# Chunked attention and a squared-ReLU layer on one core: q and k transposes issued together, and the attention output transposed by DMA from the sixth group on

## The chip, the core and the metric

The kernel runs on one core of a Trainium2 chip. A core has TensorE (PE, matmuls; its weight loads, PEld, run beside them), VectorE (DVE), ScalarE (ACT), GpSimd (POOL) and SyncE (SP, which here only issues DMAs). The engines run side by side and wait for each other through semaphores. The metric is the device time in microseconds (us), a median over runs.

## What is computed

Attention within chunks of 64 tokens, then a two-layer network on every token:

```python
# q, k, v: (8 batches, 8 heads, 576 tokens, 64), float32
scores = scale * q_chunk @ k_chunk.T            # per head, chunk by chunk: 64 x 64
attn   = softmax(scores)
x      = (attn @ v_chunk) as (4608 tokens, 8 heads * 64 = 512)
h      = maximum(x @ w_in, 0)                   # w_in 512 x 2048
out    = (h * h) @ w_out                        # w_out 2048 x 512, out (4608, 512) float32
```

## The kernel before, in words

**Groups and blocks.** The 4608 tokens are cut into 18 groups of 256 (two tiles of 128 tokens, t = 0 and 1). Attention is done by group, the network by block: block 0 is groups 0 to 2, blocks 1 to 7 are the pairs (3,4) to (15,16), block 8 is group 17. While a block runs through the network, the attention of the next block's groups is done in between.

**The four steps of a group's attention** (`T, SC, AV, XT` in the code):
- T, `transpose_qk`: TensorE transposes 8 pieces of q (128 x 128 each, through the identity matrix `ident`) into one half of a PSUM tile, DVE copies that half to SBUF (`qkT`); TensorE transposes 8 pieces of k into the other half, ACT copies it. The inputs are float32; the transposes read the upper two bytes of each value as bf16.
- SC, `scores`: 64 x 64 matmuls of k and q into a PSUM tile; ACT writes the exponential `e`.
- AV, `values`: for each t, matmuls of `e` with v (v carries a column of ones, which gives the sums), then on DVE a reciprocal `rec` and a multiplication, giving `x`, 128 tokens x 512 in bf16.
- XT, `transpose_x`: TensorE transposes 8 pieces of `x` into a PSUM tile, and DVE copies it into `xT` (128 features x 4 x tokens), the layout in which the network's first matmul wants it.

**The network.** `ffn_in` takes 16 steps (`ft`); each is four matmuls into a PSUM tile `ps_ffn`, a ReLU on ACT (`rl`) and a square on DVE (`gT`). `ffn_out` takes, per tile of 128 tokens, 16 matmuls into a `ps_ffn` tile, a copy on ACT (`o_sb`) and a store.

**What sets the order.** The code is written in the order in which each engine executes it; nothing reorders it afterwards. A dictionary `plan` says after which slot of a block (a slot is one `ft` of `ffn_in`, or four matmuls of `ffn_out`) which attention steps are issued; a pair block has slots 0 to 31. Each engine works through its own instructions in order, so an instruction that waits holds up those behind it on that engine. All DMAs are issued by SP, in order. At the head of block j SP issues the loads of block j+2; the stores follow in the order of the code.

**Buffers.** Attention's PSUM tiles, `ps_att`, rotate over 2 buffers; `ps_ffn` over 4; `x` over 6; `xT` over 2; `o_sb` over 4; q and k over 5 groups.

Of the kernel before, what the change touches and what calls it, by code (L numbers as in the profile page):

```python
# [10 lines left out]
BF16 = mybir.dt.bfloat16  # L11
# [5 lines left out]
def kernel(  # L17
# [9 lines left out]
    nc = tc.nc  # L27
# [6 lines left out]
    n_hp = H // 2  # L34
    n_dt = d_model // 128
    n_ft = d_ff // 128
    GT = 256
    n_grp = n_tokens // GT
    blocks = [[0, 1, 2]] + [[g, g + 1] for g in range(3, n_grp - 1, 2)] + [[n_grp - 1]]
    BT = GT * max(len(b) for b in blocks)  # L40

    const_pool = ctx.enter_context(tc.tile_pool(name="const", bufs=1))
# [3 lines left out]
    att_pool = ctx.enter_context(tc.tile_pool(name="att", bufs=3))  # L46
# [20 lines left out]
    def segments(g0, n):  # L67
        while n:
            b, s = divmod(g0, S)
            m = min(n, S - s)  # L70
            yield b, s, m
            g0 += m
            n -= m
# [3 lines left out]
    def load_qk(g):  # L77
        q_sb = in_pool.tile([128, 2, H, D], FP32, name="q_sb")
        k_sb = in_pool.tile([128, 2, H, D], FP32, name="k_sb")
        qk[g] = (q_sb, k_sb)  # L80
        for t in range(2):
            for dst, src in ((q_sb, q), (k_sb, k)):
                p = 0
                for b, s, m in segments(g * GT + t * 128, 128):
                    nc.sync.dma_start(  # L85
                        out=dst[p:p + m, t, :, :],
                        in_=src[b, :, s:s + m, :].rearrange("h s d -> s h d"))
                    p += m

    def load_v(g):  # L90

        vt = v_tiles[g % NV]
        for t in range(2):
            g0 = g * GT + t * 128
            p = 0
            for b, s, m in segments(g0, 128):
                nc.sync.dma_start(  # L97
                    out=vt[p:p + m, t, 0::2, 0:D],
                    in_=v[b, 0::2, s:s + m, :].rearrange("h s d -> s h d"))
                p += m  # L100
            for half in range(2):
                b, s = divmod(g0 + 64 * half, S)
                p = 64 * (1 - half)
                nc.sync.dma_start(  # L104
                    out=vt[p:p + 64, t, 1::2, 0:D],
                    in_=v[b, 1::2, s:s + 64, :].rearrange("h s d -> s h d"))

    def load_w_in(i):
        cols = slice(i * 256, (i + 1) * 256)
        st = wst_pool.tile([128, 1024], FP32, name="w_st").rearrange("p (a f) -> p a f", a=n_dt)  # L110
        nc.sync.dma_start(  # L111
            out=st, in_=moe_w_in[:, cols].rearrange("(a p) f -> p a f", p=128))
        nc.gpsimd.tensor_copy(out=w_in_bf[:, :, cols], in_=st)  # L113
# [8 lines left out]
    xTs = {}  # L122
# [4 lines left out]
    state = {}  # L127

    def transpose_qk(g):
        ps = ps_att.tile([128, 1024], FP32, name="ps_att")  # L130
        psb = ps.bitcast(BF16)
        qkT = att_pool.tile([128, 2, n_hp, GT], BF16, name="qkT")
        state["qkT", g] = qkT
        for which in range(2):
            srcb = qk[g][which].bitcast(BF16)
            for hp in range(n_hp):
                for i in range(2):
                    c0 = which * 1024 + hp * GT + i * 128
                    nc.tensor.transpose(  # L139
                        out=psb[:, c0:c0 + 128],  # L140
                        in_=srcb[:, i, 2 * hp:2 * hp + 2, 1::2],
                        identity=ident)
            dst = qkT[:, which]
            src = psb[:, which * 1024:(which + 1) * 1024].rearrange("c (h t) -> c h t", h=n_hp)
            if which == 0:
                nc.vector.tensor_copy(out=dst, in_=src)  # L146
            else:
                nc.scalar.copy(out=dst, in_=src)  # L148

    def scores(g):  # L150
        qkT = state.pop(("qkT", g))
        ps = ps_att.tile([128, 1024], FP32, name="ps_att")
        for hp in range(n_hp):
            for t in range(2):
                for a in range(2):
                    for p in range(2):
                        c = p ^ a
                        cols = slice(t * 128 + p * 64, t * 128 + p * 64 + 64)
                        o0 = a * 512 + hp * 128 + t * 64
                        nc.tensor.matmul(  # L160
                            out=ps[64 * c:64 * c + 64, o0:o0 + 64],
                            lhsT=qkT[64 * a:64 * a + 64, 1, hp, cols],
                            rhs=qkT[64 * a:64 * a + 64, 0, hp, cols],
                            start=True, stop=True)
        e = att_pool.tile([128, 2, n_hp, 2, 64], BF16, name="e")
        state["e", g] = e
        nc.scalar.activation(  # L167
            out=e.rearrange("p a h t q -> p (a h t q)"), in_=ps, func=AF.Exp, scale=scale)
# [26 lines left out]
    def transpose_x(g):  # L195
        j, c = place[g]
        if j not in xTs:
            xTs[j] = att_pool.tile([128, n_dt, BT], BF16, name="xT", bufs=2)
        ps = ps_att.tile([128, 1024], FP32, name="ps_att")
        psb = ps.bitcast(BF16)  # L200
        for t in range(2):
            x = state.pop(("x", g, t))
            for hp in range(n_hp):
                c0 = hp * GT + t * 128
                nc.tensor.transpose(  # L205
                    out=psb[:, c0:c0 + 128],
                    in_=x[:, hp].rearrange("p a d -> p (a d)"),
                    identity=ident)
        nc.vector.tensor_copy(  # L209
            out=xTs[j][:, :, c:c + GT],  # L210
            in_=psb[:, 0:1024].rearrange("p (h t) -> p h t", h=n_hp))

    T, SC, AV, XT = transpose_qk, scores, values, transpose_x

    gTs = {}

    def ffn_in(j, c, n):
        if j not in gTs:
            gTs[j] = ffn_pool.tile([128, n_ft, BT], BF16, name="gT")
        gT, xT = gTs[j], xTs[j]  # L220
        for ft in range(n_ft):
            h = ps_ffn.tile([128, 512], FP32, name="ps_ffn")
            for dt in range(n_dt):
                nc.tensor.matmul(  # L224
                    out=h[:, 0:n],
                    lhsT=w_in_bf[:, dt, ft * 128:(ft + 1) * 128],
                    rhs=xT[:, dt, c:c + n],
                    start=(dt == 0), stop=(dt == n_dt - 1))
            rl = ffn_pool.tile([128, 512], BF16, name="rl", bufs=3)
            nc.scalar.activation(out=rl[:, 0:n], in_=h[:, 0:n], func=AF.Relu)  # L230
            nc.vector.tensor_tensor(  # L231
                out=gT[:, ft, c:c + n], in0=rl[:, 0:n], in1=rl[:, 0:n], op=ALU.mult)
            yield
# [19 lines left out]
    def load(g):  # L253
        load_qk(g)
        load_v(g)

    load(0)
    load(1)
    load_w_in(0)
    load_w_in(1)  # L260
    load(2)
    for i in range(2, 8):
# [10 lines left out]
    for j, grps in enumerate(blocks):  # L273
        if j + 2 < len(blocks):
            for g in blocks[j + 2]:
                load(g)
        nxt = blocks[j + 1] if j + 1 < len(blocks) else []
        if j == 0:
            a, b = nxt
            plan = {3: [(T, 2)], 6: [(SC, 2)], 10: [(AV, 2)], 14: [(XT, 2)],  # L280
                    44: [(T, a)], 46: [(T, b)], 48: [(SC, a), (SC, b)],
                    50: [(AV, a)], 52: [(AV, b)], 54: [(XT, a)], 55: [(XT, b)]}
            phases = [ffn_in(0, 0, 512), ffn_in(0, 512, 256), ffn_out(0)]
        else:
            if len(nxt) == 2:
                a, b = nxt
                plan = {1: [(T, a)], 4: [(T, b)], 9: [(SC, a), (SC, b)], 14: [(AV, a)],
                        18: [(AV, b)], 22: [(XT, a)], 26: [(XT, b)]}
            elif nxt:
                a, = nxt  # L290
                plan = {1: [(T, a)], 6: [(SC, a)], 14: [(AV, a)], 20: [(XT, a)]}
            else:
                plan = {}
            phases = [ffn_in(j, 0, len(grps) * GT), ffn_out(j)]
        slot = 0
        for phase in phases:
            for _ in phase:
                for f, g in plan.get(slot, []):
                    f(g)
                slot += 1  # L300
# [30 lines left out]
```

## Time and profile before

| | |
|---|---|
| median of 3 runs | 353.45 us (352.02 to 353.71) |
| the profiled execution | 352.24 us, of which the span from the first to the last instruction is 350.2 us |
| TensorE matmul busy | 303.3 us, 87% of the span |
| TensorE weight loads busy | 157.9 us, 45% |
| ACT / DVE / POOL busy | 142.7 / 120.7 / 18.6 us |
| DMA | 46.58 MB in 125278 packets, mean 133 GB/s |

The windows below are stretches of the span that begin and end where a block does on TensorE:

| stretch, us | what runs | length, us |
|---|---|---|
| 0 to 57.8 | loads, attention of groups 0 to 2, `ffn_in` of block 0 | 57.8 |
| 57.8 to 85.8 | `ffn_out` of block 0, attention of groups 3 and 4 | 28.00 |
| 85.8 to 125.87 | block 1, attention of groups 5 and 6 | 40.07 |
| 125.87 to 300.97 | blocks 2 to 6, two groups' attention in each | five of 35.00 to 35.07 |
| 300.97 to 332.37 | block 7, attention of group 17 | 31.40 |
| 332.37 to 350.2 | block 8 | 17.83 |

In the rows of the profile, "busy" is time in which an engine executes, and "idle before" is the gap ahead of an instruction on its engine, with the instruction that ended the gap behind an arrow.

### The profile page before, as it was taken

Reading aid. Unit: us, or ns where it says so; the run is one execution under the profiler, and the core shown is the slowest. Engines: PE = TensorE matmul, PEld = TensorE weight load, DVE = VectorE, ACT = ScalarE, POOL = GpSimd, SP = SyncE. Lnnn points to the kernel's source line nnn. Section 1 sums busy time; section 2 is a strip of 40 time slices with the busy share of each in tenths; the row PEclk is TensorE's granted clock in tenths of the full one; section 3 lists DMA queues with packets and bytes.
Section 4 is the critical chain, followed back from the end, with each engine's and each line's share of the span. In section 5 each row is a group of like instructions: output and inputs, shape, how many; then the busy total and the mean of one; then the engine's idle time right before and its main releaser. Section 6 shows DMA issues by size and latency. Waiting matters only on the chain.

```text
span 350.2 us, 6792 instructions
## 1 busy us (share of the span) xinstructions
PE 303.3 (87%) x2800; PEld 157.9 (45%) x2800; DVE 120.7 (34%) x268; ACT 142.7 (41%) x233; POOL 18.6 (5%) x28
## 2 busy tenths in 40 slices
PE   2456979989589988998899889988998899899995
PEld 1322447444244544454445444544454445444472
DVE  0322395015235314531453145314531453144050
ACT  0323545250455146514651465146514651473171
POOL 1021681000000000000000000000000000000000
PEclk9999899999699999999999999999999999999999
DMA  9997998998992159414861586159615601100101
GB/s 168 193 229 217 366 362 179 200 172 172 278 187 48 60 140 199 85 62 117 183 122 62 135 168 121 63 136 171 115 62 138 104 2 60 62 0 31 60 32 60
DMA packets 125278, 46.58 MB, mean 133 GB/s; under 512 B 114496, under 2 KB 118592, under 8 KB 125248
## 3 DMA queue, kind: packets, MB, share of 16 engines
q1 hardware_dynamic: 125248, 46.15, 56.9%
q8 instruction: 22, 0.36, 0.5%
q14 instruction: 8, 0.07, 0.1%
HBM read 36.70 MB, written 9.44 MB: 132 GB/s over the span
## 4 chain that ended last, share of the span: by engine, by line
PE 78%; SPq 8%; DVE 6%; ACT 3%; DMA 2%; issue 1%; POOL 0%; ACTq 0%
PE ps_ffn L240 36%; PE ps_ffn L224 35%; SPq L85 3%; PE ps_att L139 3%; DVE gT L231 3%; DVE qkT L146 3%; ACT rl L230 3%; SPq L104 2%; PE ps_att L205 2%; SPq L97 2%; PE ps_att L179 2%; PE ps_att L160 2%; DMA w_st<-in_moe_w_in_dram 1%; DMA out_dram<-o_sb 1%; SPq L111 1%
## 5 line engine op out<-in xcount | busy, mean ns | idle before, releaser
L224 PE MATMUL ps_ffn<-xT,w_in_bf 128*128 128x512 bf16 (+1 forms) x640 | 137.5, 369 | 6.1 <-DVE xT L209 4.0
L240 PE MATMUL ps_ffn<-w_out_bf,gT 128*128 128x512 bf16 x576 | 130.0, 379 | 0.0
L231 DVE TENSOR_TENSOR gT<-rl 128x512 bf16<-128x512 bf16 (+1 forms) x160 | 68.0, 428 | 136.2 <-ACT rl L230 131.6
L230 ACT ACTIVATE rl<-ps_ffn 128x512 bf16<-128x512 f32 (+1 forms) x160 | 87.5, 557 | 45.2 <-PE ps_ffn L224 42.7
L224 PEld LDWEIGHTS <-w_in_bf 128*128 128x128 bf16 x640 | 62.0, 100 | 66.1 <-issue 8.8
L240 PEld LDWEIGHTS <-gT 128*128 128x128 bf16 x576 | 55.0, 98 | 62.0
L247 ACT COPY o_sb<-ps_ffn 128x512 f32<-128x512 f32 x36 | 21.1, 586 | 113.4 <-PE ps_ffn L240 103.7
L139 PE MATMUL ps_att<-ident,k_sb 128*128 128x128 bf16 x144 | 12.2, 233 | 23.9 <-DVE qkT L146 23.9
L148 ACT COPY qkT<-ps_att 128x1024 bf16<-128x1024 bf16 x18 | 18.2, 1012 | 35.5 <-PE ps_att L139 35.5
L209 DVE COPY xT<-ps_att 128x1024 bf16<-128x1024 bf16 x18 | 12.4, 691 | 38.7 <-PE ps_att L205 38.7
L189 DVE TENSOR_TENSOR x<-ps_att,rec 128x512 bf16<-128x512 f32 x36 | 24.9, 692 | 1.2
L139 PEld LDWEIGHTS <-k_sb 128*128 128x128 bf16 x144 | 10.5, 104 | 26.3 <-issue 15.7
L146 DVE COPY qkT<-ps_att 128x1024 bf16<-128x1024 bf16 x18 | 12.3, 686 | 21.4 <-PE ps_att L139 21.4
L167 ACT ACTIVATE e<-ps_att 128x1024 bf16<-128x1024 f32 x18 | 17.6, 1023 | 2.1 <-PE ps_att L160 2.1
L139 PE MATMUL ps_att<-ident,q_sb 128*128 128x128 bf16 x144 | 12.0, 229 | 6.2 <-DMA q_sb<-in_q_dram 6.2
L139 PEld LDWEIGHTS <-q_sb 128*128 128x128 bf16 x144 | 10.2, 103 | 10.3 <-DMA q_sb<-in_q_dram 6.3
L186 DVE RECIPROCAL rec<-ps_att 128x8 f32<-128x8 f32 x36 | 7.2, 201 | 22.0 <-PE ps_att L179 22.0
L205 PE MATMUL ps_att<-ident,x 128*128 128x128 bf16 x144 | 12.2, 229 | 2.2 <-DVE x L189 2.2
L205 PEld LDWEIGHTS <-x 128*128 128x128 bf16 x144 | 9.9, 101 | 6.8 <-DVE x L189 3.0
L179 PEld LDWEIGHTS <-e 64*64 64x64 bf16 x576 | 6.5, 111 | 9.3 <-issue 5.5
L179 PE MATMUL ps_att<-v_sb,e 64*64 64x65 bf16 x576 | 8.6, 200 | 2.3 <-ACT e L167 2.3
L113 POOL CAST w_in_bf<-w_st 128x1024 bf16<-128x1024 f32 x8 | 8.8, 1096 | 32.7 <-DMA w_st<-in_moe_w_in_dram 32.7
(12 smaller groups left out, 24.6 us busy)
## 6 DMA issues: line engine op xcount, KB each, us to landing
out_dram<-o_sb SPq DMA_DIRECT2D x36, 256.0 KB, 2.0
q_sb<-in_q_dram SPq DMA_DIRECT2D x32, 256.0 KB, 4.3
k_sb<-in_k_dram SPq DMA_DIRECT2D x32, 256.0 KB, 4.8
v_sb<-in_v_dram SPq DMA_DIRECT2D x80, 64.0 KB, 3.0
v_sb<-in_v_dram SPq DMA_DIRECT2D x32, 128.0 KB, 4.5
w_st<-in_moe_w_in_dram SPq DMA_DIRECT2D x8, 512.0 KB, 5.7
w_st<-in_moe_w_out_dram SPq DMA_DIRECT2D x8, 512.0 KB, 6.3
q_sb<-in_q_dram SPq DMA_DIRECT2D x8, 128.0 KB, 3.6
```

What stands on the lines that cost most here:

```text
L139: nc.tensor.transpose(out=psb[:, c0:c0 + 128], in_=srcb[:, i, 2 * hp:2 * hp + 2, 1::2], identity=ident)
L146: nc.vector.tensor_copy(out=dst, in_=src)
L148: nc.scalar.copy(out=dst, in_=src)
L167: nc.scalar.activation(out=e.rearrange("p a h t q -> p (a h t q)"), in_=ps, func=AF.Exp, scale=scale)
L179: nc.tensor.matmul(out=ps[64 * p:64 * p + 64, a, hp * (D + 1):(hp + 1) * (D + 1)], lhsT=e[64 * c:64 * c + 64, a, hp, t, :], rhs=vb[64 * c: ...
L189: nc.vector.tensor_tensor(out=x.rearrange("p h a d -> p a h d"), in0=o[:, :, :, 0:D], in1=rec.to_broadcast([128, 2, n_hp, D]), op=ALU.mult)
L205: nc.tensor.transpose(out=psb[:, c0:c0 + 128], in_=x[:, hp].rearrange("p a d -> p (a d)"), identity=ident)
L224: nc.tensor.matmul(out=h[:, 0:n], lhsT=w_in_bf[:, dt, ft * 128:(ft + 1) * 128], rhs=xT[:, dt, c:c + n], start=(dt == 0), stop=(dt == n_dt ...
L230: nc.scalar.activation(out=rl[:, 0:n], in_=h[:, 0:n], func=AF.Relu)
L231: nc.vector.tensor_tensor(out=gT[:, ft, c:c + n], in0=rl[:, 0:n], in1=rl[:, 0:n], op=ALU.mult)
L240: nc.tensor.matmul(out=o_ps, lhsT=gT[:, ft, tt * 128:(tt + 1) * 128], rhs=w_out_bf[:, ft, :], start=(ft == 0), stop=(ft == n_ft - 1))
L247: nc.scalar.copy(out=o_sb, in_=o_ps)
```

## The change

Three edits.

1. In T, all 16 transposes of a group are issued first and the two copies after them. The PSUM columns and `qkT` change their layout (t before head pair), so that both copies read and write 1024 elements in one run; SC reads `qkT` accordingly.
2. From group 5 on (`FIRST_DMA_X = 5`), XT is two DMA transposes issued by SP, each from `x` of 128 tokens x 512 straight into `xT`; the eight TensorE transposes and the DVE copy of these 13 groups are gone. The plan issues XT right behind AV.
3. At the start, q and k of groups 0 and 1 are loaded first, then v of group 0, the first piece of w_in, and v of group 1.

```diff
+    FIRST_DMA_X = 5
...
-        qkT = att_pool.tile([128, 2, n_hp, GT], BF16, name="qkT")
+        qkT = att_pool.tile([128, 2, 2, n_hp, 128], BF16, name="qkT")
...
-                    c0 = which * 1024 + hp * GT + i * 128
+                    c0 = which * 1024 + i * 512 + hp * 128
...
-            dst = qkT[:, which]
-            src = psb[:, which * 1024:(which + 1) * 1024].rearrange("c (h t) -> c h t", h=n_hp)
+        for which in range(2):
+            dst = qkT[:, which].rearrange("c t h q -> c (t h q)")
+            src = psb[:, which * 1024:(which + 1) * 1024]
...
+        if g >= FIRST_DMA_X:
+            for t in range(2):
+                x = state.pop(("x", g, t))
+                nc.sync.dma_start_transpose(
+                    out=xTs[j][:, :, c + t * 128:c + (t + 1) * 128],
+                    in_=x.rearrange("p h a d -> p (h a d)"))
+            return
...
-    load(0)
-    load(1)
+    load_qk(0)
+    load_qk(1)
+    load_v(0)
     load_w_in(0)
+    load_v(1)
     load_w_in(1)
     load(2)
...
-                plan = {1: [(T, a)], 4: [(T, b)], 9: [(SC, a), (SC, b)], 14: [(AV, a)],
-                        18: [(AV, b)], 22: [(XT, a)], 26: [(XT, b)]}
+                plan = {1: [(T, a)], 4: [(T, b)], 9: [(SC, a), (SC, b)], 14: [(AV, a), (XT, a)],
+                        18: [(AV, b), (XT, b)]}
...
-                plan = {1: [(T, a)], 6: [(SC, a)], 14: [(AV, a)], 20: [(XT, a)]}
+                plan = {1: [(T, a)], 6: [(SC, a)], 14: [(AV, a), (XT, a)]}
```

Where the instructions stand, by the order of the built programs (names in brackets are what an instruction waits for: `DVE`, `PE`, `Activation` are those engines, `DMAHW` is an earlier DMA; a line number of the changed kernel is one to nine higher than before).

TensorE before, at T(7) in block 2: the last transposes of q and the first of k (each is a weight load and a matmul).

```order
L139 LDWEIGHTS q_sb
L139 MATMUL ps_att<-ident,q_sb 128x128
L139 LDWEIGHTS k_sb [waits DMAHW5_49]
L139 MATMUL ps_att<-ident,k_sb 128x128 [waits DVE_49]
L139 LDWEIGHTS k_sb [waits DMAHW7_49]
```

TensorE now, at the same place.

```order
L140 LDWEIGHTS q_sb
L140 MATMUL ps_att<-ident,q_sb 128x128
L140 LDWEIGHTS k_sb [waits DMAHW3_49]
L140 MATMUL ps_att<-ident,k_sb 128x128
L140 LDWEIGHTS k_sb [waits DMAHW5_49]
```

The wait for DVE, which is q's copy, is gone from the first transpose of k; what is left is the wait for k's load.

ACT before, from the first ReLUs of a pair block to the exponentials.

```order
L230 ACTIVATE rl<-ps_ffn 128x512 [waits DVE_49,PE_49] x2
L148 COPY qkT<-ps_att 128x1024 [waits DVE_49,PE_49]
L230 ACTIVATE rl<-ps_ffn 128x512 [waits PE_49,Activation_49] x3
L148 COPY qkT<-ps_att 128x1024 [waits DVE_49,PE_49]
L230 ACTIVATE rl<-ps_ffn 128x512 [waits PE_49,Activation_49] x3
```

ACT now, at the same place.

```order
L239 ACTIVATE rl<-ps_ffn 128x512 [waits DVE_49,PE_49] x2
L150 COPY qkT<-ps_att 128x1024 [waits DVE_49]
L239 ACTIVATE rl<-ps_ffn 128x512 [waits PE_49,Activation_49] x3
L150 COPY qkT<-ps_att 128x1024 [waits DVE_49]
L239 ACTIVATE rl<-ps_ffn 128x512 [waits PE_49,Activation_49] x3
```

The order on ACT is the same, and k's copy still waits for DVE; it no longer waits for TensorE by itself.

SP before, between the last loads at the head of block 1 and the first loads at the head of block 2 (names of v's buffers carry a number).

```order
L97 DMA v_sb_93<-in_v_dram 128x4x64 [waits DMAHW3_49,PE_49]
L104 DMA v_sb_93<-in_v_dram 64x4x64 [waits DMAHW4_49,PE_49]
L104 DMA v_sb_93<-in_v_dram 64x4x64 [waits DMAHW5_49,PE_49]
L249 DMA out_dram<-o_sb 128x512 [waits DMAHW6_49,Activation_49]
L249 DMA out_dram<-o_sb 128x512 [waits DMAHW7_49,Activation_49]
```

SP now, from the same load on.

```order
L98 DMA v_sb_93<-in_v_dram 128x4x64 [waits DMAHW3_49,PE_49]
L105 DMA v_sb_93<-in_v_dram 64x4x64 [waits DMAHW4_49,PE_49]
L105 DMA v_sb_93<-in_v_dram 64x4x64 [waits DMAHW5_49,PE_49]
L204 DMA_TRANSPOSE xT<-x 128x4x128 [waits DMAHW6_49,DVE_49]
L204 DMA_TRANSPOSE xT<-x 128x4x128 [waits DMAHW7_49,DVE_49]
L204 DMA_TRANSPOSE xT<-x 128x4x128 [waits DMAHW0_49,DVE_49]
L204 DMA_TRANSPOSE xT<-x 128x4x128 [waits DMAHW1_49,DVE_49]
L258 DMA out_dram<-o_sb 128x512 [waits DMAHW2_49,Activation_49]
```

Four DMA transposes, each waiting for its `x` on DVE and for the eighth DMA before it, stand behind the block's loads and ahead of its stores.

More of the change, by code (lines that the diff above doesn't have):

```diff
@@ L157, in scores @@
                         c = p ^ a
-                        cols = slice(t * 128 + p * 64, t * 128 + p * 64 + 64)
+                        cols = slice(p * 64, p * 64 + 64)
                         o0 = a * 512 + hp * 128 + t * 64
@@ L161, in scores @@
                             out=ps[64 * c:64 * c + 64, o0:o0 + 64],
-                            lhsT=qkT[64 * a:64 * a + 64, 1, hp, cols],
-                            rhs=qkT[64 * a:64 * a + 64, 0, hp, cols],
+                            lhsT=qkT[64 * a:64 * a + 64, 1, t, hp, cols],
+                            rhs=qkT[64 * a:64 * a + 64, 0, t, hp, cols],
                             start=True, stop=True)
```

## The prediction

> **What bounds the kernel now.** I read the windows by block first, then the groups of the costliest lines, then TensorE's timeline of one steady block, and the chain of waits through it. The windows give length, busy time and number of instructions by engine, granted clock (PEclk) and DMA share.
>
> ```profile
> 57.80:85.80 28.00, 25.65 (x275) 13.27 (x274) 6.82 (x15) 6.76 (x10) 0.00 (x0) 1.00 0.93 175
> 85.80:125.87 40.07, 35.17 (x304) 17.22 (x304) 12.62 (x28) 15.77 (x25) 0.00 (x0) 0.91 0.58 142
> 125.87:160.88 35.01, 32.35 (x305) 16.32 (x304) 12.62 (x28) 15.29 (x24) 0.00 (x0) 1.00 0.57 121
> ...
> 265.90:300.97 35.07, 32.41 (x305) 16.28 (x304) 12.62 (x28) 15.29 (x24) 0.00 (x0) 1.00 0.34 76
> 300.97:332.37 31.40, 30.10 (x217) 14.43 (x216) 9.61 (x22) 13.63 (x22) 0.00 (x0) 1.00 0.09 34
> ```
>
> In block 2 TensorE is busy 32.35 of 35.01 us; DVE has 12.62, ACT 15.29, the DMA engines 0.57 of the time. TensorE is the bound, and 2.66 us of a steady block are its gaps. The groups say whose they are:
>
> ```profile
> L139 PE MATMUL ps_att<-ident,k_sb 128*128 128x128 bf16 x144 | 12.2, 233 | 23.9 <-DVE qkT L146 23.9
> L148 ACT COPY qkT<-ps_att 128x1024 bf16<-128x1024 bf16 x18 | 18.2, 1012 | 35.5 <-PE ps_att L139 35.5
> ```
>
> The transposes of k waited 23.9 us in 18 groups, all of it for DVE's copy of q. TensorE's timeline of block 2 (start, length, what; in brackets the gap before) shows two such gaps, and the two transposes of x:
>
> ```profile
> 125.87 1.89 PE L224 MATMUL ps_ffn<-xT,w_in_bf 128*128 128x512 bf16 x8
> 127.60 0.61 PE L139 MATMUL ps_att<-ident,q_sb 128*128 128x128 bf16 x8
> 129.51 0.61 PE L139 MATMUL ps_att<-ident,k_sb 128*128 128x128 bf16 x8 [1.30 <-DVE qkT L146]
> 129.95 2.75 PE L224 MATMUL ps_ffn<-xT,w_in_bf 128*128 128x512 bf16 x12
> 132.54 0.61 PE L139 MATMUL ps_att<-ident,q_sb 128*128 128x128 bf16 x8
> 134.51 0.61 PE L139 MATMUL ps_att<-ident,k_sb 128*128 128x128 bf16 x8 [1.36 <-DVE qkT L146]
> 134.95 4.48 PE L224 MATMUL ps_ffn<-xT,w_in_bf 128*128 128x512 bf16 x20
> ...
> 152.22 0.61 PE L205 MATMUL ps_att<-ident,x 128*128 128x128 bf16 x8
> 152.67 3.62 PE L240 MATMUL ps_ffn<-w_out_bf,gT 128*128 128x512 bf16 x16
> 156.12 0.61 PE L205 MATMUL ps_att<-ident,x 128*128 128x128 bf16 x8
> 156.57 4.48 PE L240 MATMUL ps_ffn<-w_out_bf,gT 128*128 128x512 bf16 x20
> ```
>
> The chain of waits tells why k waits so long: q's copy stands on DVE behind the square of the step before, which waits for ACT's ReLU.
>
> ```profile
> 127.80 0.61 ACT rl L230
> ...
> 128.43 0.43 DVE gT L231
> 128.85 0.61 DVE qkT L146
> ...
> 129.51 0.61 PE ps_att L139 x8
> ```
>
> **The change, part by part: steady blocks.** From T's first transpose to the network's next matmul takes 129.95 - 127.60 = 2.35 us, and the second time 134.95 - 132.54 = 2.41. Eight transposes without a wait take 0.45 (152.22 to 152.67), so sixteen take 0.90. The first edit gives 1.45 + 1.51 = 2.96 us a block, more than the gaps of 2.66, because the drain of the pipeline at each gap goes too. The second edit takes the two runs of x off TensorE, 0.90 us. Together 3.86 us: a steady block takes 35.01 - 3.86 = 31.15. Five blocks: 19.30 us.
>
> Does something else become late? k's copy still waits for q's. With block 2's times from the block's start: ReLU 1 ends at 2.54, square 1 at 2.99, q's copy at 3.59, k's copy (1.01 us) at 4.6, ReLU 2 at 5.2. TensorE has four `ps_ffn` buffers; issuing without a gap it needs the buffer of step 2 for step 6, at 7 us (1.73 for two steps, 0.90, three steps of 0.86, 0.90, 0.86). The second k copy, after ReLU 4 and its square, ends near 8.5, ReLU 5 at 9.1, and step 9 needs that buffer at 9.6. So both new waits on ACT are hidden by the buffers, by 1.7 and 0.5 us. The 13 removed copies of `xT` on DVE and the contiguous copies of T are costed at nothing: DVE is idle for over half of a block.
>
> **Block 0's end and block 1.** T(3) and T(4) run in block 0:
>
> ```profile
> 69.05 0.61 PE L139 MATMUL ps_att<-ident,q_sb 128*128 128x128 bf16 x8
> 70.44 0.61 PE L139 MATMUL ps_att<-ident,k_sb 128*128 128x128 bf16 x8 [0.78 <-DVE qkT L146]
> 70.88 1.89 PE L240 MATMUL ps_ffn<-w_out_bf,gT 128*128 128x512 bf16 x8
> ...
> 87.50 0.61 PE L139 MATMUL ps_att<-ident,q_sb 128*128 128x128 bf16 x8
> 91.65 1.01 PE L139 MATMUL ps_att<-ident,k_sb 128*128 128x128 bf16 x8 [3.54 <-DVE qkT L146]
> 92.46 5.18 PE L224 MATMUL ps_ffn<-xT,w_in_bf 128*128 128x512 bf16 x12
> 97.48 0.61 PE L139 MATMUL ps_att<-ident,q_sb 128*128 128x128 bf16 x8
> ...
> 99.94 4.48 PE L224 MATMUL ps_ffn<-xT,w_in_bf 128*128 128x512 bf16 x20
> ```
>
> T(3) takes 70.88 - 69.05 = 1.83 and will take 0.90; T(4) has the same gap of 0.78: 2 x 0.93 = 1.86 us.
>
> Block 1 has a gap of 3.54 us, and after it matmuls at half pace: 12 in 5.02 us, against 12 in 2.59 in block 2 (129.95 to 132.54); the granted clock of this window is 0.91. The cause lies on SP: the stores of block 0 stand behind 43 loads, so that ACT gets a free `o_sb` only at 88.17.
>
> ```profile
> 88.17 0.59 ACT L247 COPY o_sb<-ps_ffn 128x512 f32<-128x512 f32 x1 [9.46 <-PE ps_att L139]
> 50.83 7.16 PE L224 MATMUL ps_ffn<-xT,w_in_bf 128*128 128x256 bf16 x64 [2.42 <-DVE xT L209]
> ```
>
> (The arrow on ACT names a transpose; by the order of the code it waits for the first store to land.) The DMA share is 0.93 until 85.8, so this time stays where it is. T(5) begins at 87.50 - 1.86 = 85.64 and ends at 86.54; the next matmul needs the `ps_ffn` buffer that this ACT copy frees at 88.76, so TensorE waits until 88.85, a gap of 2.31. The gap of 2.42 at 50.83 was followed by matmuls at full pace (64 of half width in 7.0 us), so I take full pace: 12 matmuls to 91.44, T(6) to 92.34, then about 1.2 us of ACT's backlog (two k copies and two `o_sb` copies in its way) at step 9: 93.5 where it was 99.94, that is 6.4 us, of which 1.86 are block 0's. Block 1 gives 4.54, and its two runs of x 0.90.
>
> [...]
>
> **Block 7 and the end.** T(17) 1.45 and XT(17) 0.45: 1.90. Block 8 has no attention beside it: nothing.
>
> **The start.** TensorE waits there for w_in:
>
> ```profile
> 32.16 0.61 PE L139 MATMUL ps_att<-ident,k_sb 128*128 128x128 bf16 x8 [1.30 <-DVE qkT L146]
> 34.84 4.27 PE L224 MATMUL ps_ffn<-xT,w_in_bf 128*128 128x512 bf16 x12 [2.07 <-POOL w_in_bf L113]
> ...
> 8.21 0.60 SPq L85 DMA_DIRECT2D q_sb<-in_q_dram  x1
> ...
> 10.67 0.93 SPq L85 DMA_DIRECT2D k_sb<-in_k_dram  x1
> ```
>
> The piece that ends the wait stands behind the same loads as before. v of group 0 comes later by four loads, which took from 8.21 to 11.60 on SP; AV(0) may be up to 3.4 us later, and 1.30 + 2.07 us ahead of 34.84, plus the gaps in T(0) and T(1) that go, cover it. Gain and loss 0; without any cover it would be a loss of 3.4 us.
>
> **The DMA transposes.** No run shows one. Rows for the bounds:
>
> ```profile
> 141.68 1.97 SPq L104 DMA_DIRECT2D v_sb<-in_v_dram  x2
> 149.88 0.69 DVE L189 TENSOR_TENSOR x<-ps_att,rec 128x512 bf16<-128x512 f32 x1
> v_sb<-in_v_dram SPq DMA_DIRECT2D x32, 128.0 KB, 4.5
> q1 hardware_dynamic: 125248, 46.15, 56.9%
> ```
>
> Each moves 128 x 512 x 2 bytes = 128 KB, as much as a load of v, which lands 4.5 us after issue. The ordinary DMAs took 0.569 x 16 x 350.2 us / 125248 = 25.5 ns per packet. In pieces of 256 bytes (what 128 tokens give one row of `xT`) a transpose is 512 packets, 0.82 us over 16 engines; element by element it is 65536, 104 us. I take the row with the same bytes: about 1 us of SP and of the DMA engines each, 4.5 us to land. SP has finished its loads at 143.65, 17.8 us into block 2. The last `x` is ready at 150.57, 24.7 into the block, without the 2.96 of T's gaps 21.7. Two transposes from there land by 21.7 + 1 + 4.5 = 27.2; the next block's first matmul wants them at 31.15. They are hidden with 3.9 us to spare. While SP waits for an `x`, this block's stores stand behind it, with four `o_sb` buffers as cover, and the next loads, which T wants a block later. [...]
>
> **The sum.** 1.86 + 4.54 + 0.90 + 19.30 + 1.90 = 28.5 us off the profiled execution's 352.24 (a span of 350.2, and 2.04 around it): 323.7. That execution lies 0.34% under the median of 353.45; scaled to the median, 324.8.
>
> **Rivals.**
> [...]
> - k's copy, held on ACT until q's is done, uses up the `ps_ffn` buffers, and TensorE waits at step 6 or 9. If each of 13 T's in blocks 1 to 7 gave back one k copy (1.01 us), 13 us: 338 as a median. The calculated reserve of 0.5 us at step 9 speaks for a part of it, the 1.7 at step 6 against the whole.
> - Transposes that queue one behind the other at P us each: the stall is 17.8 + 4P - 31.15 per block, before six blocks. It begins at P = 3.3; at 4 it is 2.65 a block, 16 us: 341.
> - Slower than before: the same with P above 4.5, where 6 x (4P - 13.35) eats the 28.5. That is so if pieces smaller than 256 x 0.82 / 4.5 = 46 bytes are moved at 25.5 ns each: at 32 bytes P is 6.5, the stall 76 us, about 400. For it: a transpose turns rows into columns, and nothing in the trace shows in what pieces. Against it: it is an instruction of its own, DMA_TRANSPOSE, not a copy with a rearranged pattern.
>
> **Chances and range.** The forecast 0.48, the clock's drop 0.20, ACT's buffers 0.14, queued transposes short of break-even 0.10, slower 0.06; 0.02 for about no change. About 0.5% is what a measurement of this kernel can tell from no change. Faster 0.92, the same 0.02, slower 0.06. The range from 320 (block 1 and the start a little better) to 338 (all of ACT's case) leaves out the last three cases and little else.
>
> **What would show it.** k's transposes follow q's with no gap; the copy of k on ACT begins where q's on DVE ends; steady blocks of 31.15 us with no gap of TensorE for ACT's ReLU; each DMA_TRANSPOSE issued about 18 and 22 us into a block, landing within 5 us, and `ffn_in`'s first matmul not waiting for it; block 1 with a gap of about 2.3 us at 86.5 and a clock near 1.00; the first matmul after w_in's third piece still at 34.8. The prediction is wrong if TensorE waits for `xT` at the head of a block, or if the stores fall behind so far that ACT waits for `o_sb`.

## The result, and the profile after

The changed kernel takes 324.89 us (median of 4 runs, 323.69 to 326.32) against 352.96 us before (median of 4 runs: the three of the table above and a fourth): a ratio of 0.921, 95% interval 0.916 to 0.925. The forecast was 324.8. The profiled execution took 326.32 us, a span of 324.5: the trace below is that of the slowest of the four, 1.4 us above the median, while the profiled execution of before, 352.24 us, lies 0.7 below its median. Read against the forecast for the profiled execution, 323.7, the change fell short by 2.6 us, and the terms below say where.

A trace misses some matmul records, so a row may count 11 matmuls where 12 were issued. The windows of the changed kernel, cut where the blocks begin, as before (length, busy time of PE, PEld, DVE, ACT and POOL, granted clock, DMA share, GB/s):

```profile
56.22:82.30 26.08, 24.88 (x270) 13.16 (x273) 7.28 (x16) 6.89 (x11) 0.00 (x0) 1.00 0.87 178
82.30:121.51 39.21, 33.82 (x284) 16.36 (x288) 11.32 (x26) 15.36 (x25) 0.00 (x0) 0.91 0.83 177
121.51:152.65 31.14, 30.88 (x284) 15.37 (x288) 11.23 (x26) 14.85 (x24) 0.00 (x0) 1.00 0.65 153
...
246.24:277.38 31.14, 30.88 (x285) 15.32 (x289) 11.24 (x26) 14.84 (x24) 0.00 (x0) 1.00 0.45 103
277.38:306.88 29.50, 29.29 (x206) 13.91 (x209) 8.94 (x21) 13.41 (x22) 0.00 (x0) 1.00 0.14 45
```

A steady block went from 35.01 to 31.14 us, and TensorE is now busy for 30.88 of them. Block 1 hardly moved: 40.07 to 39.21, and its clock is still 0.91.

The groups that answer to those of before, k's transposes and the copy of k:

```profile
L140 PE MATMUL ps_att<-ident,k_sb 128*128 128x128 bf16 x144 | 12.1, 230 | 0.2 <-DMA k_sb<-in_k_dram 0.2
L150 ACT COPY qkT<-ps_att 128x1024 bf16<-128x1024 bf16 x18 | 18.2, 1012 | 35.0 <-DVE qkT L148 35.0
```

The 23.9 us of TensorE's waits for DVE are gone; the 0.2 us left are for a load of k. ACT stands idle ahead of its copies of k for about as long as before, 35.0 us (35.5), but what ends that wait is now q's copy on DVE instead of TensorE. TensorE's timeline of block 2, and ACT's two k copies in it, show both sides:

```profile
121.51 1.89 PE L233 MATMUL ps_ffn<-xT,w_in_bf 128*128 128x512 bf16 x7
123.24 0.61 PE L140 MATMUL ps_att<-ident,q_sb 128*128 128x128 bf16 x8
123.68 0.61 PE L140 MATMUL ps_att<-ident,k_sb 128*128 128x128 bf16 x8
124.13 2.75 PE L233 MATMUL ps_ffn<-xT,w_in_bf 128*128 128x512 bf16 x12
...
125.13 1.01 ACT L150 COPY qkT<-ps_att 128x1024 bf16<-128x1024 bf16 x1 [1.09 <-DVE qkT L148]
128.71 1.01 ACT L150 COPY qkT<-ps_att 128x1024 bf16<-128x1024 bf16 x1 [1.09 <-DVE qkT L148]
129.62 2.24 ACT L239 ACTIVATE rl<-ps_ffn 128x512 bf16<-128x512 f32 x4
```

From T's first transpose to the next matmul it is now 0.89 us (2.35 before), and ACT's waits of 1.09 leave no gap on TensorE.

The DMA transposes, by issue and landing, by SP's time (minimum, median and maximum in ns), in SP's timeline of block 2, and the queue's totals:

```profile
xT<-x SPq DMA_TRANSPOSE x26, 2.5
...
L204 SPq DMA_TRANSPOSE xT<-x x26: 1188/1216/2428, 108.0 to 295.2; - x26
...
140.69 5.17 SPq L204 DMA_TRANSPOSE xT<-x  x4
...
q1 hardware_dynamic: 139392, 49.56, 67.6%
```

Each holds SP for 1.22 us and lands 2.5 us after its issue. The queue moved 139392 - 125248 = 14144 packets more than before, 544 per transpose, and its engines were busy for 0.676 x 16 x 324.5 - 0.569 x 16 x 350.2 = 322 us more, which is 0.77 us of all 16 per transpose. This is an estimate, since the time of the other DMAs differs between executions too: the same subtraction gives 0.60 us for the run with every transpose twice less the changed kernel (0.719 x 16 x 326.9 - 0.676 x 16 x 324.5 = 251 us) and 0.71 for three times less twice (0.704 x 16 x 360.0 for three times).

Block 1, where the forecast missed; TensorE, then SP's first stores of block 0 and the ACT copy that waits for them:

```profile
84.02 0.61 PE L140 MATMUL ps_att<-ident,q_sb 128*128 128x128 bf16 x8
84.47 0.61 PE L140 MATMUL ps_att<-ident,k_sb 128*128 128x128 bf16 x8
90.09 0.58 PE L233 MATMUL ps_ffn<-xT,w_in_bf 128*128 128x512 bf16 x1 [5.01 <-ACT o_sb L256]
90.89 4.47 PE L233 MATMUL ps_ffn<-xT,w_in_bf 128*128 128x512 bf16 x10 [0.22 <-issue]
95.16 1.03 PE L140 MATMUL ps_att<-ident,q_sb 128*128 128x128 bf16 x8
...
86.86 4.30 SPq L258 DMA_DIRECT2D out_dram<-o_sb  x6
...
89.45 0.59 ACT L256 COPY o_sb<-ps_ffn 128x512 f32<-128x512 f32 x1 [14.21 <-DMA out_dram<-o_sb]
```

T(5) came early, the store late, the gap of TensorE is 5.01 us, and the 12 matmuls after it take 95.16 - 90.09 = 5.07 us, half pace: the granted clock is 0.50 from 89.21 to 96.04 us.

### The profile page after: what moved, and what is told of

It reads as the page before. It is cut to its first block, busy times and chain, and to the rows that moved or that the text cites. A ratio compares the mean times of both kernels' runs of the same rounds, so it can differ in the third digit from the quotient of the medians.

```text
span 324.5 us, 6598 instructions
## 1 busy us (share of the span) xinstructions
PE 291.5 (90%) x2655; PEld 151.5 (47%) x2696; DVE 112.7 (35%) x255; ACT 139.3 (43%) x233; POOL 18.3 (6%) x28
## 2 busy tenths in 40 slices
DMA packets 139421, 49.97 MB, mean 154 GB/s; under 512 B 128640, under 2 KB 132736, under 8 KB 139392
## 3 DMA queue, kind: packets, MB, share of 16 engines
q1 hardware_dynamic: 139392, 49.56, 67.6%
## 4 chain that ended last, share of the span: by engine, by line
PE 76%; SPq 13%; DMA 7%; issue 2%; POOL 1%; ACT 0%; DVE 0%; ACTq 0%
PE ps_ffn L249 35%; PE ps_ffn L233 33%; SPq L86 7%; PE ps_att L140 4%; SPq L105 3%; SPq L98 2%; DMA v_sb<-in_v_dram 2%; DMA w_st<-in_moe_w_in_dram 2%; DMA w_st<-in_moe_w_out_dram 2%; PE ps_att L181 2%; PE ps_att L162 2%; DMA out_dram<-o_sb 1%; SPq L112 1%; ACT o_sb L256 0%; POOL w_out_bf L121 0%
## 5 line engine op out<-in xcount | busy, mean ns | idle before, releaser
L233 PE MATMUL ps_ffn<-xT,w_in_bf 128*128 128x512 bf16 (+1 forms) x611 | 133.9, 365 | 11.9 <-ACT o_sb L256 5.0
L249 PE MATMUL ps_ffn<-w_out_bf,gT 128*128 128x512 bf16 x564 | 126.7, 379 | 0.8 <-issue 0.3
L240 DVE TENSOR_TENSOR gT<-rl 128x512 bf16<-128x512 bf16 (+1 forms) x160 | 68.7, 435 | 154.2 <-ACT rl L239 149.1
L239 ACT ACTIVATE rl<-ps_ffn 128x512 bf16<-128x512 f32 (+1 forms) x160 | 84.5, 559 | 33.0 <-PE ps_ffn L233 30.1
L181 PE MATMUL ps_att<-v_sb,e 64*64 64x65 bf16 x576 | 9.5, 200 | 5.0 <-DMA v_sb<-in_v_dram 3.7
L162 PE MATMUL ps_att<-qkT 64*64 64x64 bf16 x576 | 7.3, 199 | 3.7 <-ACT qkT L150 3.7
L140 PEld LDWEIGHTS <-k_sb 128*128 128x128 bf16 x144 | 9.6, 104 | 0.4 <-DMA k_sb<-in_k_dram 0.4
L162 PEld LDWEIGHTS <-qkT 64*64 64x64 bf16 x576 | 6.0, 112 | 8.1 <-ACT qkT L150 4.2
L121 POOL CAST w_out_bf<-w_st 128x1024 bf16<-128x1024 f32 x8 | 8.7, 1084 | 2.1 <-DMA w_st<-in_moe_w_out_dram 2.0
```

Of the source, the lines that this page charges most:

```text
L140: nc.tensor.transpose(out=psb[:, c0:c0 + 128], in_=srcb[:, i, 2 * hp:2 * hp + 2, 1::2], identity=ident)
L162: nc.tensor.matmul(out=ps[64 * c:64 * c + 64, o0:o0 + 64], lhsT=qkT[64 * a:64 * a + 64, 1, t, hp, cols], rhs=qkT[64 * a:64 * a + 64, 0, t, ...
L181: nc.tensor.matmul(out=ps[64 * p:64 * p + 64, a, hp * (D + 1):(hp + 1) * (D + 1)], lhsT=e[64 * c:64 * c + 64, a, hp, t, :], rhs=vb[64 * c: ...
L233: nc.tensor.matmul(out=h[:, 0:n], lhsT=w_in_bf[:, dt, ft * 128:(ft + 1) * 128], rhs=xT[:, dt, c:c + n], start=(dt == 0), stop=(dt == n_dt ...
L240: nc.vector.tensor_tensor(out=gT[:, ft, c:c + n], in0=rl[:, 0:n], in1=rl[:, 0:n], op=ALU.mult)
L249: nc.tensor.matmul(out=o_ps, lhsT=gT[:, ft, tt * 128:(tt + 1) * 128], rhs=w_out_bf[:, ft, :], start=(ft == 0), stop=(ft == n_ft - 1))
```

## The experiments

Two theories stood at the start. Mine: TensorE's time is the sum, the gaps in T and the transposes of x were on the path, everything else is hidden, except that block 1 is held by block 0's first store. The rivals: the time of T's gaps comes back as waits on ACT; the DMA transposes delay loads or stores; and the start's 1.6 us (T(3) began at 67.45 instead of 69.05, which the forecast did not have) belong to the order of the loads.

### One edit at a time

The first edit alone (`FIRST_DMA_X` out of reach, plan and loads as before).

> Only the first edit: the 16 transposes of q and k together, copies after them; x still transposed on TensorE at its old slots, loads in the old order. Theory (TensorE's gaps were the time, edits add up): 2.96 us in each of five steady blocks, 1.86 in block 0, 1.45 in block 7, and the 1.6 us that the start gained in the changed kernel, since that start has no gap in T(2) any more: about 333 us. Rival (the gaps come back as waits for ACT's k copy, and the gain of the whole change came from x): under 8 us gained, 345 us or more. Rival on the start: the start's 1.6 us belong to the order of the loads, so T(3) begins at 69 as before.

Measured: 329.17 us, ratio 0.936 (0.929 to 0.942). The rival is out. It is 4 us faster than I expected, since I had left block 1's 4.54 us out of that sum; with them, and without the start's 1.6, it is 352.75 - 22.65 = 330.1. A steady block takes 32.04 us here, 2.97 less than before (2.96 expected). And here block 1 went much as the forecast of the whole change had it:

```profile
86.01 0.61 PE L140 MATMUL ps_att<-ident,q_sb 128*128 128x128 bf16 x8
...
88.17 2.75 PE L233 MATMUL ps_ffn<-xT,w_in_bf 128*128 128x512 bf16 x11 [1.10 <-ACT o_sb L256]
90.75 0.61 PE L140 MATMUL ps_att<-ident,q_sb 128*128 128x128 bf16 x8
...
96.14 1.02 PE L233 MATMUL ps_ffn<-xT,w_in_bf 128*128 128x512 bf16 x4 [0.83 <-ACT rl L239]
```

A short gap, 12 matmuls in 2.58 us at full pace, and then a wait of 0.83 us for ACT's backlog at step 9, forecast at 1.2. T(3) began at 69.44 us in this trace, without the start's gain.

The second edit alone (DMA transposes and plan, T and the loads as before).

> Only the second edit: x of groups 5 to 17 transposed by DMA, issued right behind AV; q and k and the loads as before. Theory: 0.45 us for each of 13 groups come off TensorE and nothing else moves: 5.85 us, about 347. Rival (the DMA transposes delay stores or loads): no gain or a loss, 352 or more, with ACT waiting for o_sb or SP late with the loads.

Measured: 346.54 us, ratio 0.984 (0.977 to 0.991), 6.2 us for an expected 5.85, with an interval that reaches from 3 to 8 us. The steady blocks say it more sharply: 34.12 us each, 0.89 less than before (0.90 expected). The two edits together give 2.97 + 0.89 = 3.86 us a block; the whole change gave 3.87.

The third edit alone.

> Only the third edit: the order of the first loads. Theory: nothing on the path, 353 within 1.5 us; T(3) begins at 69 us, and the first store of block 0 is issued near 85.7. Rival: this order gave the start's 1.6 us (T(3) at 67.4), or delays the stores of block 0 by the 1.15 us by which they came later in the changed kernel (86.9).

Measured: 351.88 us, ratio 1.000 (0.997 to 1.004): no time in it. But T(3) began at 66.87 in this trace, and at 66.42 in that of the second edit alone, which has the old loads. Both have a gap over 7 us in block 1 (TensorE, two rows of the second edit alone, then one of the third):

```profile
92.90 1.01 PE L140 MATMUL ps_att<-ident,k_sb 128*128 128x128 bf16 x8 [7.42 <-DVE qkT L147]
...
94.56 2.81 PE L232 MATMUL ps_ffn<-xT,w_in_bf 128*128 128x512 bf16 x10 [0.22 <-issue]
...
93.29 1.01 PE L139 MATMUL ps_att<-ident,k_sb 128*128 128x128 bf16 x8 [7.35 <-DVE qkT L146]
```

So where the start is early, block 1 waits longer for the store: in these traces the start's 1.6 us are no gain that is kept. The complement, edits 1 and 2 without the third:

> The changed kernel with the first loads in the old order (edits 1 and 2 without 3). Theory (the third edit is not on the path, and what the start gains or loses is taken up by the wait for block 0's first store): 323 to 327, as the changed kernel; the network's first matmul near 24.5 us where it is 27.3, T(3) anywhere from 66 to 69. Rival (edit 3 makes the stores of block 0 land 1.2 us later): 2 us faster, 322.

Measured: 325.22 us, ratio 0.920 (0.915 to 0.925), as the changed kernel. The network began at 24.28 instead of 27.3 us, then waited 4.43 us for w_in where the changed kernel waits 1.23, T(3) began at 70.14, and the gap in block 1 was shorter:

```profile
35.88 0.86 PE L233 MATMUL ps_ffn<-xT,w_in_bf 128*128 128x512 bf16 x3 [4.43 <-POOL w_in_bf L114]
...
91.16 0.59 PE L233 MATMUL ps_ffn<-xT,w_in_bf 128*128 128x512 bf16 x1 [3.40 <-ACT o_sb L256]
```

The first store was issued at 87.84 with the old loads here, at 87.11 with them in the second edit alone, and at 85.0 with them in the first edit alone: its time differs by 3 us between traces with the same order of loads. Over all twelve traces T(3) begins between 66.4 and 70.1 us with the old order (five traces) and between 66.9 and 69.0 with the new (seven), and the first store is issued between 85.0 and 87.8 and between 86.2 and 88.0: neither tells the two orders apart.

### Block 1's wait

The changed kernel with more room for outputs:

```diff
-                    o_sb = ffn_pool.tile([128, d_model], FP32, name="o_sb", bufs=4)
+                    o_sb = ffn_pool.tile([128, d_model], FP32, name="o_sb", bufs=6)
```

> The changed kernel with 6 o_sb buffers in place of 4, so that ACT need not wait for block 0's stores, which stand on SP behind the loads. Theory (in block 1 the gap of 5.0 us and the half pace after it come from that wait): the gap goes, and with it the slow clock, 5.0 + 2.4 us: about 317.5, granted clock of the block 1 window near 1.00. Rival (TensorE in block 1 is held by the loads themselves, DMA share 0.9): the wait moves to AV(5), AV(6) or to xT at the head of block 2, 322 to 325.

Measured: 319.81 us, ratio 0.907 (0.900 to 0.914), against 0.921 (0.916 to 0.925) for the changed kernel: the fastest version of this study. The window of block 1, and T(5) with the matmuls after it:

```profile
83.80:115.28 31.48, 31.09 (x284) 15.27 (x288) 11.23 (x26) 14.38 (x24) 0.00 (x0) 1.00 0.78 189
...
85.99 0.61 PE L140 MATMUL ps_att<-ident,k_sb 128*128 128x128 bf16 x8
86.44 2.75 PE L233 MATMUL ps_ffn<-xT,w_in_bf 128*128 128x512 bf16 x11
...
49.25 8.66 PE L233 MATMUL ps_ffn<-xT,w_in_bf 128*128 128x256 bf16 x64 [2.34 <-DVE xT L218]
```

Gap and slow clock are both gone, and block 1 is a steady block, though the first store went out no earlier (87.39). That shows the wait for `o_sb` as the cause. The time is 5.1 us lower, not the 7.4 that I expected from the profiled execution, which was 1.4 us above its median; T(3) began 1.5 us later in this one. The last row shows why: after a gap of only 2.34 us in block 0, 64 matmuls of half width took 8.66 us. The granted clock of this trace from 0 to 56 us is 0.97 on average (1.00 in the changed kernel, to 56.22), by estimate 0.03 x 56 / 0.5 = 3.4 us at half pace. In seven other traces (before, the changed kernel, each edit alone, the old loads, three `ps_ffn` buffers) the gap at this place, 1.52 to 2.53 us, was followed by full pace (7.16 to 7.22 us).

The same with the old order of the loads:

> The changed kernel with 6 o_sb buffers and the first loads in the old order. Theory (the order of the first loads is not on the path): 318 to 321, as with 6 buffers alone. Rival (the old order lets the network start 2.5 us earlier, and without the wait for block 0's stores this is kept): 317.

Measured: 321.6 us, 0.6 above the expected range, ratio 0.912 (0.905 to 0.920); the interval overlaps that of the new order. The granted clock of its profiled execution is 1.00: no slow stretch in it. Whether either is faster by under 1% stays open.

### What hides the DMA transposes

Each transpose twice, and three times (`range(2)`), the extra ones into a scratch tile:

```diff
+                for _ in range(1):
+                    sc = att_pool.tile([128, n_dt, 128], BF16, name="xscr", bufs=4)
+                    nc.sync.dma_start_transpose(
+                        out=sc, in_=x.rearrange("p h a d -> p (h a d)"))
                 nc.sync.dma_start_transpose(
                     out=xTs[j][:, :, c + t * 128:c + (t + 1) * 128],
```

> The changed kernel with every DMA transpose issued twice (the extra one into a scratch tile): 8 a block. Theory, with the measured 1.2 us of SP each and 1.3 from the end of the issue to landing: begun 19.2 us into the block, the last lands at 19.2 + 8 x 1.2 + 1.3 = 30.1, before the next block's first matmul at 31.15: no change, 324 to 327. Rival (transposes take more of the DMA engines than SP's time shows, or delay the stores): 330 or more.

> Every DMA transpose issued three times: 12 a block. Theory: the last lands at 19.2 + 12 x 1.2 + 1.3 = 34.9, so TensorE waits 3.8 us at the head of blocks 2 to 7, six times, 23 us, and up to 2.4 us more each where the clock drops after it: 347 to 362. Rival (DMA engines work several transposes at a time, so that SP's order does not limit): under 330.

Measured: twice, 327.12 us, ratio 0.930 (0.922 to 0.937), 0.1 us above the expected range; the interval overlaps the changed kernel's, and TensorE waited for `xT` once in the whole trace, 1.39 us. Three times, 362.72 us, ratio 1.031 (1.024 to 1.038), 0.7 us above the expected range. TensorE's idle time by what ended it (us, times), and two windows from one block's first matmul to the next's:

```profile
  DMA xT<-x: 27.0, 6
...
124.30:161.41 37.11, 32.47 (x283) 15.67 (x289) 11.22 (x26) 14.85 (x24) 0.00 (x0) 0.96 0.73 159
161.41:199.91 38.50, 32.58 (x284) 15.88 (x290) 11.31 (x26) 14.88 (x24) 0.00 (x0) 0.95 0.72 152
```

Six waits of 4.1 to 5.5 us, 4.5 on average, one at the head of each of blocks 2 to 7, where the arithmetic of SP's queue gave 3.8: in block 2 twelve transposes took SP 15.65 us, 1.30 each, not 1.2. Most of the rest of the loss is the clock, 0.96 and 0.95 in the two blocks shown: TensorE is busy for 32.5 us in them, 1.6 to 1.7 more than in the changed kernel. Eight transposes fit into a block of this kernel, twelve do not: that is the margin of the change. The forecast's rivals of queued transposes have their mechanism right, but their sum is too small. With the 15.65 us for 4P it gives a stall of 17.8 + 15.65 - 31.15 = 2.3 us a block and a kernel faster than before; measured are 4.5 us and a kernel 3% slower. The sum leaves out the time to landing, a queue that begins 20.0 us into the block in this trace and not at 17.8, and the clock after each wait.

From group 3 on instead of group 5:

```diff
-    FIRST_DMA_X = 5
+    FIRST_DMA_X = 3
```

> The changed kernel with FIRST_DMA_X = 3: x of groups 3 and 4 also by DMA, from block 0, where the DMA engines are busy with loads and SP issues 20 loads of the next block ahead of them. Theory (a DMA transpose is hidden only if SP and the DMA engines are free in time): SP comes to these four transposes at about 86.9, where it now issues the first store, and block 1's first matmul, now at 82.3, waits for them until about 87 + 4 x 1.2 + 1.3 = 93; the stores and the wait for o_sb move 5 us later too, to about 94.5 + 0.6, against 90.1: 4 to 10 us slower than the changed kernel, 329 to 335. Rival (hidden as the others are): 0.45 us a group gained, 324.

Measured: 335.7 us, ratio 0.954 (0.947 to 0.962), slower than the changed kernel by 11, and 0.7 us above the expected range. The mechanism was the one expected, its size was not: the wait ended at 97.71, not at 93. TensorE at the head of block 1, and SP ahead of it:

```profile
97.71 2.72 PE L233 MATMUL ps_ffn<-xT,w_in_bf 128*128 128x512 bf16 x6 [17.28 <-DMA xT<-x]
...
86.94 3.42 SPq L258 DMA_DIRECT2D out_dram<-o_sb  x5
90.45 2.64 SPq L204 DMA_TRANSPOSE xT<-x  x2
93.18 0.53 SPq L258 DMA_DIRECT2D out_dram<-o_sb  x1
93.81 2.52 SPq L204 DMA_TRANSPOSE xT<-x  x2
```

In block 0 XT is written behind five stores, and the fifth waits for ACT, which waits for the first to land. I had put the transposes ahead of the stores; behind them they begin at 90.45, not 86.9.

### What hides ACT's waits

The changed kernel with one `ps_ffn` buffer less:

```diff
-    ps_ffn = ctx.enter_context(tc.tile_pool(name="ps_ffn", bufs=4, space=bass.MemoryType.PSUM))
+    ps_ffn = ctx.enter_context(tc.tile_pool(name="ps_ffn", bufs=3, space=bass.MemoryType.PSUM))
```

> The changed kernel with 3 ps_ffn buffers in place of 4. Theory (the new waits on ACT for the copies of k are hidden by the buffers): with 3, step 8 of a pair block needs the buffer that ReLU 5 frees at about 9.1 us at 8.7, a wait of 0.4 us, and block 1, which has ACT's backlog, 1 to 3 us: 2 to 8 us slower than with 4, 327 to 333, TensorE's gaps in a steady block standing behind ACT's ReLU. Rival (the buffers do not matter, ACT keeps up in any case): no change, 325.

Measured: 327.96 us, ratio 0.929 (0.924 to 0.934). The total fits, though the intervals touch; half of the reason does not. A stretch as long as a steady block, from the last 2.8 us of block 1 on, and block 1:

```profile
121.50:152.65 31.15, 30.89 (x284) 15.28 (x288) 11.23 (x26) 14.79 (x25) 0.00 (x0) 1.00 0.67 153
...
91.27 1.86 PE L233 MATMUL ps_ffn<-xT,w_in_bf 128*128 128x512 bf16 x4 [6.79 <-ACT o_sb L256]
```

Steady blocks wait for nothing even with three buffers; the cost lies in block 1, where TensorE stops one step earlier: from its first matmul to the end of T(6) it takes 15.75 us (83.45 to 99.20), against 14.18 in the changed kernel (82.30 to 96.48). Another 1.15 us of this trace were lost before block 1, where T(3) began later. Steady blocks are free of waits because the copies of k are hidden with more to spare than the forecast's 0.5 us: by the rows of ACT in block 2 of the changed kernel, ReLU 5 ends at about 129.62 + 0.6, which is 8.7 us into the block and not 9.1. With four buffers about 0.9 us are left at step 9; with three, step 8 needs the buffer at 8.7 and gets it just in time.

## Why the prediction was right, and where its steps were off

The span by its pieces, in the two profiled executions (from T's first transpose to T's first transpose, with the rows of both traces):

| piece | before, us | after, us | gained | forecast |
|---|---|---|---|---|
| start to T(3) | 69.05 | 67.45 | 1.60 | 0 |
| T(3) to T(5), block 0's end | 18.45 | 16.57 | 1.88 | 1.86 |
| T(5) to the end of T(6), block 1 | 12.44 | 12.46 | 0.0 | 4.54 |
| end of T(6) to T(7) | 27.66 | 26.76 | 0.90 | 0.90 |
| T(7) to T(17), five blocks | 175.10 | 155.86 | 19.24 | 19.30 |
| T(17) to block 8 | 29.67 | 27.77 | 1.90 | 1.90 |
| block 8 | 17.83 | 17.62 | 0.2 | 0 |
| sum | 350.2 | 324.5 | 25.7 | 28.5 |

- **Steady blocks, blocks 0 and 7**: right to 0.1 us. What made them so was counting from start to start (2.35 to 0.90) and not by the gaps, which would have given 0.3 us a block less.
- **The DMA transposes**: right as hidden, with the price in the range. 512 packets were estimated, 544 measured; 0.82 us of the engines, 0.60 to 0.77 by the runs; about 1 us of SP, 1.22 measured; 4.5 us to landing, 2.5 measured. In block 2 SP issued the four one behind the other, 19.2 to 24.4 us into the block, so that the last landed near 25.6, where 27.2 was worked out. By the landing they are faster than v's 128 KB (from DRAM) in the same trace, 2.5 us against 4.0; 128 KB in 0.60 to 0.77 us of all engines is, by estimate, 170 to 220 GB/s.
- **Block 1** is the term that was mis-sized: 4.54 us forecast, none in the profiled execution. Its step that failed is "this time stays where it is" together with a start costed at zero. T(5) began at 84.02 (forecast 85.64) and the buffer came free at 90.04 (forecast 88.76), so the gap was 5.01 us instead of 2.31, and the clock dropped, to which the forecast gave a chance of 0.20: 5.07 us for 12 matmuls, 2.48 more than at full pace. The forecast case exists, in the first edit alone, where the gap was 1.10 and the pace full. The mechanism held: in the five traces where T(5) has both runs of transposes together and waits for `o_sb` (the changed kernel, the first edit alone, the old loads, the transposes twice and three times) the gap is the first store's issue less the start of T(5) plus 2.1 us, to within 0.2: 5.01, 1.10, 3.40, 4.66 and 3.73 us. What failed is that both times were taken as fixed; each differs by 3 us or more between the traces, T(3) from 66.4 to 70.1 and the first store from 85.0 to 88.0.
- **The clock**: to take full pace after 2.31 us because it had followed a gap of 2.42 was weak ground: after 2.34 us in the run with 6 buffers 64 matmuls took 8.66 us, not 7.16. In block 1 of the changed kernel TensorE did nothing at all in the 3.41 us before the clock fell (85.80 to 89.21). In the trace of before it fell to 0.50 at 35.93 us, soon after a gap of 2.07, and stayed at 1.00 after the gap of 2.42: the busy time in stretches of 3.41 us tells better there than the gap (the last section has the figures).
- **ACT's buffers**: right, no gap in steady blocks, with 0.9 us of reserve at step 9 where 0.5 was worked out.
- **The start**: the term was 0 and the third edit alone shows 0; T(3)'s scatter is not this change's.

That the median met the forecast to 0.1 us is partly luck: the gain was put 2.6 us too high for the execution profiled, and that execution is the slowest of the four. Within it, block 1's missing 4.5 us and the start's 1.6, which nobody forecast, partly cancel. The other three executions have no trace; their granted clocks, 0.993 to 0.995 against 0.989, would fit a shorter slow stretch, which is not shown.

## What to carry to other kernels

Where an engine in order waits in the middle of a pair of like steps, issue both halves before the first dependent copy, and price it from start to start: here that was 1.45 us for a gap of 1.30. A transfer moved to a DMA queue cost TensorE no time here as long as its place in the queue, behind every load and store ahead of it, came before its deadline (four transposes a block: no wait; eight: one of 1.39 us; twelve: six of 4.5 on average): count the issue time of the whole queue, and look where the program writes it, as starting two groups earlier cost 11 us. When a steady stage is cleared, look at the one block with another limit: here two more output buffers gave a further 5 us.

## What the runs showed of the hardware that I had not expected

- A DMA transpose of 128 KB holds the issuing engine for 1.22 us, twice the 0.60 of most loads of v, and lands in 2.5 us, faster than a load of 128 KB of v (4.0 us).
- How long the half pace lasts after a gap does not follow from the gap's length: in the changed kernel 10 matmuls took 4.47 us soon after a gap of 5.01; in the second edit alone, after a longer gap of 7.42 and k's transposes, 10 took 2.81. In the trace of before the granted clock was 0.50 from 35.93 to 39.34 us and from 90.54 to 97.37, in that of the changed kernel from 89.21 to 96.04, where TensorE had work again 0.9 us after the fall. The slow stretches last 3.41, 6.83 and 6.83 us, and the full clock between the two of before 51.20, which is 15 x 3.413.
- Cut into stretches of 3.41 us at these changes, the two traces have 173 at full clock, from 29.10 us (before) and 31.18 (changed kernel) to the end of TensorE's work. After three of them the clock fell to 0.50, and TensorE had been busy in them for 1.34 us (before, 32.52 to 35.93), 0.98 (before, 87.13 to 90.54) and 0 (changed kernel, 85.80 to 89.21). After the other 170, each with 2.05 us or more, it stayed at 1.00. Transposes are part of these times: of the 1.34 us other matmuls took 1.09, and of the 2.05 us at 97.37 to 100.78 (before), after which the clock stayed, 1.11. That speaks for transposes counting as work here; stretches this close in other matmuls do not prove it.
